# A decode kernel's first weight load in eight pieces of 16 partitions, and w3 in one load behind w2

## The chip, the cores and the metric

The kernel runs on one core of a Trainium2 chip (eight cores on two dies). The metric is the device time of the program in microseconds; the median of three runs before the change is 1324.46 us (1324.42 to 1324.49).

The core has five engines with a queue of instructions each: PE (TensorE, matrix products), DVE (VectorE), ACT (ScalarE), POOL (GpSimd) and SP (SyncE), which here only issues DMA transfers. The transfers run on 16 DMA engines of the core. SBUF is the working memory with 128 partitions; PSUM holds the results of PE.

## The reference

One decode step of two branches that are mixed by a gate. Branch A is attention of one query token against a long key and value cache, branch B a small gated mixer with two dense layers. The batch is 2, the model width 1024, there are 32 heads of 128 with 16384 cached positions each, and F is 3584. All inputs are bf16.

```
x = A_x                                            # [2, 1, 1024]
g = sigmoid((x * gate_w).sum(-1))

# A: q = x @ wq, attention over the caches, then @ wo
q = (x @ wq).reshape(B, 1, 32, 128)
scores = einsum(q, k_cache) * 128 ** -0.5
a = (softmax(scores) @ v_cache).reshape(B, 1, 4096) @ wo

# B: with one token, the shifted pieces of h are padding
h  = gelu(layernorm(x) @ w1)
x1 = x + shifted(h) @ w2
b  = x1 + gelu(layernorm(x1) @ w3) @ w4

out = g * a + (1 - g) * b
```

With one token per sequence every shift moves h out of the window, so shifted(h) is zero and w1 isn't read.

## The kernel before

All large operands go through one SBUF tensor, `ring`, of five slots with 128 partitions and 32 KB per partition each (`SLOT` is 16384 bf16 numbers). A block of the K or V cache is a pair of heads of one batch entry: 128 rows of 64 KB, which fills two slots. There are 32 such pairs, and so 32 K loads (L358) and 32 V loads (L362). V uses slots 0 and 1; K alternates between slots 2, 3 and 3, 4.

The weights use the same slots before the first pair: wq slots 0 and 1, w2 slot 2, w3 slots 3 and 4, and w4 slots 0 and 1 again once the q product has read wq. `runs` (L327 to L332) makes one such load: partition p gets rows r0 to r0 + rn of its own eight (or 28) rows of the weight, one contiguous run for each of the 128 partitions. wo comes behind the last V.

SP issues all ring loads, in the order of a list. `queue_load` appends to it and `pump` moves its head to SP's program as soon as the slots that it needs have a known release; the load then waits for the event that ends the last use of those slots. A load that is marked `more` takes slots that its predecessor already holds, and waits for nothing. The order before is: the first row of w3 for each partition (0.9 MB, key `("w3", "first")`), wq (8.4 MB), w2 (2.1 MB), rows 1 to 7 of w3 (6.4 MB, `more`), w4 (7.3 MB, waits for the q product), then K, V, K, V and so on. Each load adds to a semaphore of its first slot (`s_ring`) when it lands. Loads in several pieces, which only wo has, use one semaphore for each piece (`s_tail`).

On PE the prologue is fixed: the transposes of x (L587), the q product on wq (256 small matmuls, L602, which wait for all of wq), the permutation of q (L611), the gate, the product with w2 (L507), the layer norm, the product with w3 (L474, 224 matmuls), the gelu, and the product with w4 (L507, 112 matmuls). Each product waits for its whole weight. The K block of the first pair needs slots 2 and 3: w2's product and the first five of eight steps of w3's product release them. The loop then runs 16 times over two pairs each: DVE transposes K in place (L645), PE computes the scores (L651), DVE and ACT the softmax, PE the product with V (L687).

A few small loads of x and gate_w are issued by ACT at the start (L566 to L569).

## Time and profile before

| what | value |
|---|---|
| median of 3 runs | 1324.46 us |
| the profiled execution: span from the first to the last instruction | 1323.1 us |
| bytes read from HBM | 570.44 MB, 431 GB/s over the span |
| PE busy | 780.2 us (59%) |
| DVE busy | 659.8 us (50%) |
| ACT, POOL busy | 45.7 us (3%), 23.5 us (2%) |
| chain that ended last | DMA 71%, PE 23%, DVE 6% |
| mean granted clock of TensorE | 0.801 |

The profiled execution's own time is its span of 1323.1 us and what lies around it; the runs' median is 1.4 us above that span.

The page gives busy shares of 40 equal slices of the span (33.1 us each here), the chain that ended last, and groups of instructions. The timeline lists merged instructions: start, duration, engine, line, operands, and in brackets the idle time ahead of them and what ended it. The windows view gives busy times in chosen stretches. Where it books a DMA packet, it books it whole; a 64 KB packet lasts over 2 us, so short windows of the DMA column swing around the mean. In the trace "in_B_w_dram" stands for w2, w3 and w4 alike, since numbers in names are left out; the sizes tell them apart: 896 KB is the first row of w3, 2048 KB w2, 6272 KB the rest of w3, and 7168 KB w4. The wq load is one of 8192 KB.

### The profile page before, as it was taken

The page shows a single profiled execution, that of the slowest core. Times are in us where ns is not written, and L with a number is a line of the kernel's source. Part 1 is how long each engine was busy: PE and PEld are TensorE (multiplying, and loading weights), DVE is VectorE, ACT ScalarE, POOL GpSimd, SP SyncE. Part 2 cuts the span into 40 slices and gives each one's busy share as a digit, 9 for nine tenths or more (in the row PEclk, how much of TensorE's full clock was granted, in tenths as well). Part 3 has the DMA queues.
Part 4 walks back from the last instruction along what each step waited for, and adds up shares of the span by engine and source line. Part 5 has one row for each costly group of instructions (what it writes and reads, how often), then busy time and mean ns, then how long its engine had stood idle before and what let it go on. Part 6 is the DMA issues. An engine that isn't in the chain of part 4 may idle for free.

```text
span 1323.1 us, 12311 instructions
## 1 busy us (share of the span) xinstructions
PE 780.2 (59%) x5235; PEld 333.4 (25%) x5235; DVE 659.8 (50%) x527; ACT 45.7 (3%) x99; POOL 23.5 (2%) x110
## 2 busy tenths in 40 slices
PE   1745556656456665645666564567556557756556
PEld 1622222222222222222222222222222222222223
DVE  0254446655444665544466554446655445665444
ACT  0000000000000000000000000000000000000000
POOL 3000000000000000000000000000000000000000
PEclk9976788787788878678887867888786788778679
DMA  9999999999999999999999999999999999999998
GB/s 416 433 425 437 432 434 432 436 434 434 432 434 436 430 436 436 428 442 430 428 442 430 428 442 430 428 442 430 428 442 430 430 440 430 430 440 430 432 438 367
DMA packets 11122, 570.60 MB, mean 431 GB/s; under 512 B 1236, under 2 KB 1764, under 8 KB 2023
## 3 DMA queue, kind: packets, MB, share of 16 engines
q1 hardware_dynamic: 11080, 570.43, 99.7%
q8 instruction: 8, 0.13, 0.0%
q10 hardware_dynamic: 30, 0.01, 0.0%
q14 instruction: 4, 0.02, 0.0%
HBM read 570.44 MB, written 0.00 MB: 431 GB/s over the span
## 4 chain that ended last, share of the span: by engine, by line
DMA 71%; PE 23%; DVE 6%; issue 0%; SPq 0%
DMA ring<-in_A_k_cache_dram 65%; PE ps L651 22%; DVE ring L645 6%; DMA ring<-in_B_w_dram 3%; DMA ring<-in_A_wo_dram 2%; PE ps L474 1%; SPq L331 0%; PE ps L726 0%; DVE orow L755 0%
## 5 line engine op out<-in xcount | busy, mean ns | idle before, releaser
L651 PE MATMUL ps<-ring,Z 128*128 128x512 bf16 x2048 | 531.7, 417 | 390.5 <-DVE ring L645 389.8
L645 DVE STREAM_TRANSPOSE ring<-ring 128x2048 f32<-128x2048 f32 x256 | 565.2, 2276 | 276.6 <-DMA ring<-in_A_k_cache_dram 276.6
L651 PEld LDWEIGHTS ps<-ring,Z 128*128 128x128 bf16 x2048 | 202.0, 104 | 707.5 <-issue 465.2
L687 PE MATMUL ps<-ring,PT_sb 128*32 128x512 bf16 x2048 | 167.8, 501 | 4.6 <-DVE recip L678 4.6
L701 DVE SCALAR_TENSOR_TENSOR OT_sb<-ps,gT,recip 128x2 f32 x32 | 7.0, 220 | 203.4 <-PE ps L698 203.4
L687 PEld LDWEIGHTS ps<-ring,PT_sb 128*32 128x32 bf16 x2048 | 68.3, 122 | 90.2 <-issue 69.0
L672 ACT ACTIVATE P_sb<-ps,negm 128x512 bf16<-128x512 f32 x32 | 22.0, 687 | 1007.1 <-DVE negm L670 1007.1
L661 DVE TENSOR_REDUCE rA<-ps 128x1 f32<-128x512 f32 x32 | 22.1, 692 | 64.2 <-PE ps L651 64.2
L676 PE MATMUL ps<-rowsum,hsel 128*128 128x1 f32 x128 | 23.6, 288 | 38.0 <-ACT P_sb L672 38.0
L674 DVE STREAM_TRANSPOSE PT_sb<-P_sb 128x512 bf16<-128x512 bf16 x32 | 22.8, 712 | 27.0 <-ACT P_sb L672 27.0
L632 POOL TENSOR_TENSOR Z<-q_f,mask 128x8 bf16<-128x8 f32 x64 | 12.3, 227 | 1205.8 <-PE ps L651 1205.8
L676 PEld LDWEIGHTS ps<-rowsum,hsel 128*128 128x128 f32 x128 | 20.9, 233 | 40.7 <-ACT P_sb L672 40.7
L663 PE MATMUL ps<-ident,rmax_bf 128*1 128x128 bf16 x32 | 6.9, 217 | 33.1 <-DVE rmax_bf L662 33.1
L696 ACT ACTIVATE acc_sb<-ps 128x512 bf16<-128x512 f32 x32 | 19.1, 597 | 198.5 <-PE ps L687 198.5
L698 PE MATMUL ps<-dsel,acc_sb 128*128 128x2 bf16 x128 | 8.1, 167 | 22.5 <-ACT acc_sb L696 22.5
L602 PE MATMUL ps<-xT_bf,ring 128*128 128x2 bf16 x256 | 7.1, 165 | 21.6 <-DMA ring<-in_A_wq_dram 19.3
L474 PE MATMUL ps<-xn_bf,ring 128*128 128x2 bf16 x224 | 14.4, 202 | 1.6 <-DMA ring<-in_B_w_dram 1.6
L698 PEld LDWEIGHTS ps<-dsel,acc_sb 128*128 128x128 bf16 x128 | 5.3, 96 | 38.2 <-ACT acc_sb L696 38.2
L663 PEld LDWEIGHTS ps<-ident,rmax_bf 128*1 128x1 bf16 x32 | 2.5, 79 | 48.9 <-DVE rmax_bf L662 48.9
L474 PEld LDWEIGHTS ps<-xn_bf,ring 128*128 128x128 bf16 x224 | 14.3, 162 | 1.7 <-DMA ring<-in_B_w_dram 1.7
L664 DVE TENSOR_REDUCE m_sb<-ps 1x2 bf16<-1x128 bf16 x32 | 8.9, 279 | 9.9 <-PE ps L663 9.9
L670 DVE TENSOR_SCALAR negm<-ps,cAB 128x1 f32<-128x1 f32 x32 | 8.9, 277 | 9.2 <-PE ps L667 9.2
(98 smaller groups left out, 87.2 us busy)
## 6 DMA issues: line engine op xcount, KB each, us to landing
ring<-in_B_w_dram SPq DMA_DIRECT2D x1, 7168.0 KB, 28.0
ring<-in_B_w_dram SPq DMA_DIRECT2D x1, 6272.0 KB, 43.6
ring<-in_A_wo_dram SPq DMA_DIRECT2D x1, 4096.0 KB, 38.6
ring<-in_B_w_dram SPq DMA_DIRECT2D x1, 2048.0 KB, 28.4
ring<-in_A_wo_dram SPq DMA_DIRECT2D x1, 2048.0 KB, 22.4
ring<-in_A_wo_dram SPq DMA_DIRECT2D x1, 1024.0 KB, 24.5
ring<-in_B_w_dram SPq DMA_DIRECT2D x1, 896.0 KB, 4.6
ring<-in_A_k_cache_dram SPq DMA_DIRECT2D x32, 27.0
```

Of the source, the lines that this page charges most:

```text
L474: fn = lambda e, nb=nb, kl=kl: e.matmul(out_ps[:, nb, :], lhsT=cols(wv, kl, nb, nout), rhs=rhs_of(kl), start=False, stop=True, skip_group_ ...
L632: ev = pl.add("pool", lambda e, hp=hp: e.tensor_tensor(Z[:, :, ZO:ZO + P].rearrange("p t (i c) -> p t i c", c=32)[:, :, 2 * hp:2 * hp + 2, ...
L645: return pl.add("dve", lambda e: e.transpose(ap, ap), waits=(arrived(("k", n)),), sig=True)
L651: ev = pl.add("pe", lambda e, bp=bp: e.matmul(S_ps[:, 0:NCOL], lhsT=Z[:, bp, ZO - 2 * u:ZO - 2 * u + P], rhs=kv[:, :, bp // 2, :, bp % 2], ...
L661: e1 = pl.add("dve", lambda e: e.tensor_reduce(rA[:, :], S_ps[:, 0:NCOL], axis=AX.X, op=ALU.max), waits=(ev_S[n],), sig=True)
L663: e3 = pl.add("pe", lambda e: e.transpose(mt_ps, rmax_bf[:, :], ident[:, :]), waits=(e2,), sig=True)
L672: e7 = pl.add("act", lambda e: e.activation(P_sb[:, :], S_ps[:, 0:NCOL], ACT.Exp, bias=negm[:, 0:1], scale=scale, accum_out=rowsum[:, 0:1] ...
L674: e8 = pl.add("dve", lambda e: e.transpose(PT_sb[:, :], P_sb[:, :]), waits=(e7,), sig=True)
L676: e9 = pl.add("pe", lambda e, hp=hp: e.matmul(l_ps[:, hp:hp + 1], lhsT=hsel[:, hp, :], rhs=rowsum[:, 0:1], start=True, stop=True, skip_gro ...
L687: ev = pl.add("pe", lambda e, jj=jj, cg=cg: e.matmul(acc_ps[32 * cg:32 * cg + 32, 0:512], lhsT=PT_sb[:, 32 * jj:32 * jj + 32], rhs=vv[:, 4 ...
L696: e1 = pl.add("act", lambda e: e.activation(acc_sb[:, :], acc_ps[:, 0:512], ACT.Copy), waits=(ev_pv,), sig=True)
L698: e2 = pl.add("pe", lambda e, w=w: e.matmul(oT_ps, lhsT=acc_sb[:, w * P:(w + 1) * P], rhs=dsel[:, w, :], start=(w == 0), stop=(w == 3)), w ...
```

## The change

wq becomes the first load of the list and is issued as eight loads. Load j takes partitions j, j + 8, j + 16 up to j + 120, 16 rows of 64 KB, from the same rows of wq as before into the same places. All eight use the semaphore of slot 0, and the q product waits for the sum of all eight. w3's separate first row goes, and all eight rows of w3 come in one load, 57 KB per partition, behind w2. It now waits for its slots by the ordinary rule, and they are free at the start.

```
@@ pump @@
-                    dsem = s_ring[slots[0]] if len(fns) == 1 else s_tail[k]
+                    dsem = s_ring[slots[0]] if len(fns) == 1 or key[0] == "wq" else s_tail[k]
@@ wloads @@
-        wloads[("wq", 0)] = [runs(A_wq, HD, 0, NBD)]
-        wloads[("w3", 0)] = [runs(B_w3, F, 1, NBD - 1)]
+        wloads[("wq", 0)] = [lambda e, idx, j=j: e.dma_start(
+            ring[j:P:8, idx:, :].rearrange("p s m -> p (s m)")[:, 0:NBD * HD],
+            A_wq.rearrange("(p r) n -> p (r n)", p=P)[j:P:8, :]) for j in range(8)]
+        wloads[("w3", 0)] = [runs(B_w3, F, 0, NBD)]
@@ the list @@
-        queue_load(("w3", "first"), [runs(B_w3, F, 0, 1)], w_slots["w3"])
         for key in [("wq", 0)] + w_order:
-            queue_load(key, wloads[key], w_slots[key[0]], more=key[0] == "w3")
+            queue_load(key, wloads[key], w_slots[key[0]])
```

The order of SP's instructions from the start of the program, before the change (line, operation, target and source, partitions x elements, and the engine whose semaphore it waits for; e_pe is PE's):

```order
L331 DMA ring<-in_B_w3_dram 128x3584
L331 DMA ring<-in_A_wq_dram 128x32768
L331 DMA ring<-in_B_w2_dram 128x8192
L331 DMA ring<-in_B_w3_dram 128x25088
L331 DMA ring<-in_B_w4_dram 128x28672 [waits e_pe]
L358 DMA ring<-in_A_k_cache_dram 128x32768 [waits e_pe]
```

The same place of SP's program with the change:

```order
L341 DMA ring<-in_A_wq_dram 16x32768 x8
L331 DMA ring<-in_B_w2_dram 128x8192
L331 DMA ring<-in_B_w3_dram 128x28672
L331 DMA ring<-in_B_w4_dram 128x28672 [waits e_pe]
L360 DMA ring<-in_A_k_cache_dram 128x32768 [waits e_pe]
```

The small load of w3 at the head is gone, wq stands first as eight loads of 16 rows, and from w2 on the order is as it was. The first load that waits for anything is w4, before and after.

PE's instructions at the start of the program with the change (dr0 and dr2 are the semaphores of the loads into slots 0 and 2):

```order
L588 MATMUL ps0<-ident,xg_row 128x3 [waits e_pool,dgw,dmisc]
L588 MATMUL ps0<-ident,xg_row 128x3 x7
L603 MATMUL ps1<-xT_bf,ring 128x2 [waits e_dve,dr0]
L603 MATMUL ps1<-xT_bf,ring 128x2 x255
L612 MATMUL ps2<-q_sb,PermQ 128x64 [waits e_pool,e_dve]
L612 MATMUL ps2<-q_sb,PermQ 128x64 x3
L400 MATMUL ps5<-gin,ones_f 128x2 [waits e_dve]
L509 MATMUL ps2<-ring,shT_bf 2x256 [waits dr2]
```

Nothing moved on PE: these rows are those of before but for line numbers, and the q product still waits once, for all of wq.

## The prediction

> **What bounds the kernel now.** I read the page's slices first, then the windows of the loop, then the chain that ended last, and last the timeline of the first 85 us, since the change lies there.

> ```profile
> DMA  9999999999999999999999999999999999999998
> GB/s 416 433 425 437 432 434 432 436 434 434 432 434 436 430 436 436 428 442 430 428 442 430 428 442 430 428 442 430 428 442 430 430 440 430 430 440 430 432 438 367
> DMA packets 11122, 570.60 MB, mean 431 GB/s; under 512 B 1236, under 2 KB 1764, under 8 KB 2023
> ```

> The DMA row is 9 in all slices but the last. No slice is empty, and the rate leaves 425 to 442 GB/s only in the first slice (416) and the last (367). 570.60 MB at one rate is the whole kernel: the compute engines follow.

> ```profile
> 82.15:120.85 38.70, 24.67 (x139) 10.14 (x139) 20.24 (x15) 1.38 (x3) 0.38 (x2) 0.72 1.01 434
> 1243.19:1281.89 38.70, 23.49 (x139) 9.61 (x139) 20.18 (x15) 1.38 (x3) 0.38 (x2) 0.76 1.00 434
> ```

> These are the first and the last pass of the loop (the windows view: length, then busy time of PE, PE loads, DVE, ACT, POOL, then clock, DMA share and GB/s). Both take 38.70 us at 434 GB/s, with PE busy for 24 of the 38.7 us and DVE for 20. A pass loads one K and one V block, 2 x 128 rows of 64 KB. Over the 16 DMA engines that is 16 rows each, so **one row takes 38.70 / 16 = 2.42 us on its engine**, or 27.1 GB/s. The clock of TensorE was 0.72 and 0.76 in the two passes and changed nothing. What the kernel costs is therefore: when the first byte moves, how long each engine needs for its share, and what comes behind the last byte. Work on PE matters only where a load is issued so late that the queue runs dry.

> ```profile
> 0.74 0.40 SPq L331 DMA_DIRECT2D ring<-in_B_w_dram  x1
> 1.20 0.42 SPq L331 DMA_DIRECT2D ring<-in_A_wq_dram  x1
> 1.67 33.41 SPq L331 DMA_DIRECT2D ring<-in_B_w_dram  x3
> 25.25 5.87 PE L602 MATMUL ps<-xT_bf,ring 128*128 128x2 bf16 x214 [19.29 <-DMA ring<-in_A_wq_dram]
> 34.76 0.23 DVE L607 CAST q_sb<-ps 128x64 bf16<-128x64 f32 x1 [16.75 <-PE ps L602]
> 45.34 0.17 DVE L441 TENSOR_TENSOR xn_bf<-zc,mv 128x16 bf16<-128x16 f32 x1 [0.83 <-POOL mv L439]
> 45.91 14.36 PE L474 MATMUL ps<-xn_bf,ring 128*128 128x2 bf16 x224 [1.60 <-DMA ring<-in_B_w_dram]
> 54.97 0.33 SPq L358 DMA_DIRECT2D ring<-in_A_k_cache_dram  x1
> 62.84 4.91 PE L507 MATMUL ps<-ring,GT_bf 128*2 128x256 bf16 x112 [2.58 <-DMA ring<-in_B_w_dram]
> ...
> 82.17 17.67 DVE L645 STREAM_TRANSPOSE ring<-ring 128x2048 f32<-128x2048 f32 x8 [11.55 <-DMA ring<-in_A_k_cache_dram]
> ```

> This is the timeline of the prologue. The q product waits for wq until 25.25. Its end lets SP issue w4 (the last of the x3, which ends at 1.67 + 33.41 = 35.08), 10.8 us before the w3 load in front of it lands (45.91). K of the first pair is issued at 54.97, 7.9 us before w4 lands (62.84). So the queue has at least 7.9 us of work in it whenever PE is what releases the next load.

> **The change, part by part.** The bytes are the same: w3 loses its separate first row (0.9 MB) and has all eight in one load, and wq comes as 8 x 16 rows. A term is needed for each of four things.

> *Issues on SP.* Two issues (0.40 and 0.42 us, rows above) become eight ahead of w2. At 0.46 us from one start to the next (0.74 to 1.20), w2 is issued at about 0.74 + 8 x 0.46 = 4.4 us instead of 1.67. A load of 16 rows has one row per engine, at least 2.42 us of work, so each load is issued before its predecessor is through, and w2's turn comes behind 19 us of wq. Cost 0. It would show if an issue took over 2.42 us, six times what any takes here.

> *The start of the stream.*

> ```profile
> 1.00:1.50 0.50, 0.00 (x0) 0.00 (x0) 0.00 (x0) 0.00 (x0) 0.30 (x1) 1.00 0.00 0
> 1.50:2.00 0.50, 0.00 (x0) 0.00 (x0) 0.00 (x0) 0.00 (x0) 0.41 (x2) 1.00 0.91 133
> 2.00:2.50 0.50, 0.00 (x0) 0.00 (x0) 0.00 (x0) 0.00 (x0) 0.39 (x2) 1.00 0.68 133
> 2.50:3.00 0.50, 0.00 (x0) 0.00 (x0) 0.00 (x0) 0.00 (x0) 0.39 (x3) 1.00 1.02 287
> 3.00:3.50 0.50, 0.00 (x0) 0.00 (x0) 0.00 (x0) 0.00 (x0) 0.33 (x4) 1.00 0.82 330
> 3.50:4.00 0.50, 0.00 (x0) 0.00 (x0) 0.00 (x0) 0.00 (x0) 0.50 (x1) 1.00 0.95 401
> 4.00:4.50 0.50, 0.00 (x0) 0.00 (x0) 0.00 (x0) 0.00 (x0) 0.32 (x2) 1.00 1.05 444
> ```

> In half-microsecond windows the first load, with rows of 7 KB, comes up through 133, 133, 287, 330 and 401 GB/s. Against 434 it loses (5 x 434 - 1284) x 0.5 / 434 = 1.0 us. Wide rows and short issues can save nothing at all or this 1.0 us. I take 0.4 us, since the first access is as cold as before and only the spread of the sixteen starts should shrink.

> *w2 and w3 behind wq.* w2 moves ahead of all of w3, and w3's 50 KB and 7 KB pieces become one 57 KB row. The bytes on each engine are unchanged and the loads are queued back to back: 0. What waits for them moves with them. q now waits for 2.1 us less (0.9 MB at 434), and w3 lands where it did.

> *The eight loads of 16 rows.* This is the term that decides, and no row of the trace shows a large load of fewer than 128 partitions. From below: each row takes the 2.42 us that it took, 8 rows per engine are 19.4 us, and the term is 0. That this is what wq costs now is seen here:

> ```profile
> ring<-in_B_w_dram SPq DMA_DIRECT2D x1, 896.0 KB, 4.6
> ring<-in_B_w_dram SPq DMA_DIRECT2D x1, 2048.0 KB, 28.4
> ring<-in_A_wq_dram SPq DMA_DIRECT2D x1, 24.0
> ...
> 26.00:28.00 2.00, 2.00 (x81) 2.00 (x79) 0.00 (x0) 0.00 (x0) 0.00 (x0) 1.00 1.03 443
> ```

> The first load lands at 0.74 + 4.6 = 5.3, wq at 1.20 + 24.0 = 25.2, so wq takes 19.9 us, near the 19.4. From above: if a load's rows come in by half as many ways as there are engines, two rows share each way, a row takes 4.84 us, and wq costs 8 x 2.42 = 19.4 us more. Every pass stands at the same 16 x 27.1 GB/s whatever PE and DVE do beside it, and w2 with its rows of 16 KB, which lands at 1.67 + 28.4 = 30.1 and so fills the window from 26 to 28, runs at 443, about the same. That is the picture of sixteen fixed ways of 27.1 GB/s and not of one common limit that happens to be shared. If such a way ends at an engine, the new loads still use all sixteen. If it ends at a group of partitions, it depends on which partitions a load touches: 128 rows fill all ways evenly and hide the grouping, while partitions j, j + 8, j + 16 ... all agree in their low three bits, so a grouping that uses one of those bits leaves half of the ways idle, for four loads in a row. The nearest rows, those of wq in one load, stand at the lower end, but they are no evidence for it: 128 rows look alike in both cases. I take the upper end, +19.4 us, because the spacing of eight is even for one kind of way alone, blocks of eight partitions, and uneven for every kind that deals them out more finely. Both ends stay in the range.

> [...]

> *What hangs on it.* With +19.4, wq lands near 25.25 - 2.1 - 0.4 + 19.4 = 42.1. The q product to the end of the normalization then takes the 45.34 - 25.25 = 20.1 us that it takes now, so xn_bf is there at 62.2. w3 lands at 45.91 - 0.4 + 19.4 = 64.9, still later, so PE waits for w3 as it does now. w4's issue comes at 42.1 + (35.08 - 25.25) = 51.9, 13 us ahead of w3's landing; K's and w4's times move alike. The queue stays full, the delay is neither hidden nor made larger, and everything behind it moves by one amount.

> **The sum.** The profiled execution spans 1323.1 us; the median of 1324.46 lies 1.4 us above it, which I carry along. 1323.1 - 0.4 + 19.4 + 0 + 0 + 1.4 = 1343.5, that is 1.4% slower.

> **The rivals.**

> *The same pace with 16 rows.* The ways end at the engines, every row keeps 2.42 us, and only the start moves: 1324.46 - 0.4 = 1324.1, with bounds of 1323.4 (all of the 1.0 us is saved) and 1324.5. This also decides the other sign: nothing but the start can gain, and 1.0 us is under the 0.2% (2.6 us) that a measurement of this kernel can tell from no change. For it speaks that each load has one row for each of 16 engines, and that the queue is full. Against it speaks only the regular spacing.

> *Rows dealt by partition to engines.* If it is the engine that is fixed by the partition's low bits, loads 0 to 3 give two rows each to eight engines and loads 4 to 7 to the other eight. The second eight start when the fifth load is issued, 4 x 0.46 = 1.8 us later, but each still has eight rows. The stream ends up to 1.8 us later: 1324.46 + 1.8 - 0.4 = 1325.9, within 0.2%. [...]

> *Fewer ways still.* If eight partitions apart leaves a quarter of the ways, a row takes four times 2.42 us and wq costs 3 x 19.4 = 58 us more: 1382.

> *A real gain.* Above 2.6 us it would need something ahead of the loop that is idle now, and the first two slices have no room for it.

> **How the numbers follow.** Half the ways 0.63, the same pace 0.29, dealt by partition 0.04, a quarter 0.02, a gain 0.02. Slower by over 0.2% is 0.63 + 0.02 = 0.65, within 0.2% is 0.29 + 0.04 = 0.33, faster 0.02. The likeliest case has its own range of 1342 to 1346: the start between 0 and 1.0 us of gain, and up to 10% more than a doubling where two rows compete. Since the second case holds 0.29, the range must reach down to its lower bound: 1323.4 to 1346.

> **What would show it.** If the forecast is right, the q product starts near 42 us, the w3 product near 65 us, K of the first pair lands near 101, and the second slice of GB/s falls below 300, while every pass of the loop keeps 38.70 us at 434 GB/s. If the q product starts near 22.7 us and the first K lands near 82 as now, the term of the eight loads was nothing. If q starts at 42 but the end moves by less than 19 us, something behind it gave way that I take as rigid. If the passes themselves change length, my reading that they only follow the stream is wrong.

## The result, and the profile after

The kernel with the change takes 1345.83 us (median of 5 runs, 1345.75 to 1346.02) against 1324.42 us before (5 runs, 1324.26 to 1324.49): a ratio of 1.0162, 95% interval 1.015 to 1.0174, that is 21.4 us more. The profiled execution spans 1344.5 us, before 1323.1: the same 21.4.

The page of the changed kernel, its slices and its DMA totals (as quoted of before):

```profile
DMA  9999999999999999999999999999999999999998
GB/s 219 356 427 436 429 435 435 435 437 435 429 431 437 429 435 433 435 437 437 433 427 435 437 429 433 435 435 437 437 429 429 437 433 431 435 433 437 437 435 362
DMA packets 11089, 570.60 MB, mean 424 GB/s; under 512 B 1331, under 2 KB 1859, under 8 KB 1990
```

The bytes are the same 570.60 MB. The DMA engines are as busy as before, 9 in every slice, and yet the first slice has half the rate: 219 GB/s against 416. The busy share is made up of the packets' times, and a row of wq takes 5.1 us here instead of 2.42 (below): from 27 to 42 us the share is 0.99 at 202 GB/s. So the DMA row alone hides this loss; the GB/s row shows it. From the third slice on nothing differs.

The windows view of the changed kernel, three stretches of wq, then w2 and w3, then the first and the last pass of the loop (length, busy PE, PE loads, DVE, ACT, POOL, clock, DMA share, GB/s):

```profile
7.00:22.00 15.00, 0.61 (x8) 0.56 (x8) 2.64 (x11) 1.28 (x1) 5.59 (x25) 1.00 0.92 188
22.00:27.00 5.00, 0.00 (x0) 0.00 (x0) 0.00 (x0) 0.00 (x0) 0.00 (x0) 1.00 1.06 225
27.00:42.00 15.00, 0.00 (x0) 0.00 (x0) 0.00 (x0) 0.00 (x0) 0.00 (x0) 1.00 0.99 202
...
47.00:64.00 17.00, 8.60 (x205) 7.06 (x202) 5.24 (x18) 0.17 (x1) 0.13 (x1) 1.00 1.04 445
...
103.48:142.18 38.70, 23.49 (x139) 9.60 (x139) 20.18 (x15) 1.38 (x3) 0.38 (x2) 0.76 1.00 432
1264.52:1303.20 38.68, 23.35 (x139) 9.54 (x139) 20.18 (x15) 1.37 (x3) 0.38 (x2) 0.76 1.00 434
```

While wq comes in, the rate is 188 to 225 GB/s; with w2 and w3 it is 445, and a pass of the loop keeps its 38.7 us. The loss lies between 2 and 43 us, and all behind it is only later.

The timeline of the changed kernel at the places shown of before:

```profile
0.74 5.04 SPq L341 DMA_DIRECT2D ring<-in_A_wq_dram  x8
...
5.81 48.54 SPq L331 DMA_DIRECT2D ring<-in_B_w_dram  x3
...
44.14 5.87 PE L603 MATMUL ps<-xT_bf,ring 128*128 128x2 bf16 x214 [34.98 <-DMA ring<-in_A_wq_dram]
...
64.62 0.17 DVE L443 TENSOR_TENSOR xn_bf<-zc,mv 128x16 bf16<-128x16 f32 x1 [0.83 <-POOL mv L441]
67.25 14.35 PE L476 MATMUL ps<-xn_bf,ring 128*128 128x2 bf16 x224 [3.66 <-DMA ring<-in_B_w_dram]
76.31 0.33 SPq L360 DMA_DIRECT2D ring<-in_A_k_cache_dram  x1
...
84.19 4.74 PE L509 MATMUL ps<-ring,GT_bf 128*2 128x256 bf16 x112 [2.59 <-DMA ring<-in_B_w_dram]
...
103.51 17.67 DVE L646 STREAM_TRANSPOSE ring<-ring 128x2048 f32<-128x2048 f32 x8 [11.71 <-DMA ring<-in_A_k_cache_dram]
```

The q product starts 18.9 us later (25.25 to 44.14). Most of what is missing there to 21.3 is w3's first row, 2.1 us of work that came ahead of wq before. From the w3 product on everything is 21.3 us later: 45.91 to 67.25, 54.97 to 76.31, 62.84 to 84.19, 82.17 to 103.51.

The trace also holds each DMA packet with its start and duration; here a packet is one row of wq. Medians in us of the 1st to 16th row, the 17th to 32nd and so on, in order of their start:

```
change                              4.82 5.11 5.11 5.11 4.90 5.09 5.09 5.09
wq in one load of 128 partitions    3.06 2.42 2.42 2.42 2.42 2.42 2.42 2.42
```

(The second line is the first experiment.) In the change the first sixteen rows start between 2.14 and 2.83 us, so sixteen are under way at once, and from the second load on most take 5.1 us, 2.1 times the 2.42. The fifth load (j = 4) is a little faster, 4.90; this comes up again below.

### The profile page after: what moved, and what is told of

The parts are those of the page before. It is cut to its first block, busy times and chain, and to the rows that moved or that the text cites. A ratio compares the mean times of both kernels' runs of the same rounds, so it can differ in the third digit from the quotient of the medians.

```text
span 1344.5 us, 12301 instructions
## 1 busy us (share of the span) xinstructions
PE 792.1 (59%) x5235; PEld 336.1 (25%) x5235; DVE 659.7 (49%) x527; ACT 45.7 (3%) x99; POOL 23.5 (2%) x110
## 2 busy tenths in 40 slices
DMA  9999999999999999999999999999999999999998
DMA packets 11089, 570.60 MB, mean 424 GB/s; under 512 B 1331, under 2 KB 1859, under 8 KB 1990
## 4 chain that ended last, share of the span: by engine, by line
DMA 69%; PE 23%; DVE 6%; issue 1%; SPq 0%; another core or an unknown queue 0%
DMA ring<-in_A_k_cache_dram 64%; PE ps L652 22%; DVE ring L646 6%; DMA ring<-in_A_wq_dram 3%; DMA ring<-in_A_wo_dram 2%; PE ps L476 1%; PE ps L603 1%; SPq L341 0%; DVE hsd L543 0%; PE ps L509 0%; PE ps L400 0%; SPq L331 0%; DVE orow L756 0%; PE ps L727 0%
## 5 line engine op out<-in xcount | busy, mean ns | idle before, releaser
L688 PE MATMUL ps<-ring,PT_sb 128*32 128x512 bf16 x2048 | 179.6, 528 | 4.8 <-DVE recip L679 4.8
L677 PEld LDWEIGHTS ps<-rowsum,hsel 128*128 128x128 f32 x128 | 20.8, 231 | 40.7 <-ACT P_sb L673 40.7
L603 PEld LDWEIGHTS ps<-xT_bf,ring 128*128 128x128 bf16 x256 | 7.0, 104 | 37.9 <-DMA ring<-in_A_wq_dram 35.1
## 6 DMA issues: line engine op xcount, KB each, us to landing
ring<-in_B_w_dram SPq DMA_DIRECT2D x1, 2048.0 KB, 43.0
ring<-in_A_wo_dram SPq DMA_DIRECT2D x1, 2048.0 KB, 22.6
ring<-in_A_k_cache_dram SPq DMA_DIRECT2D x32, 27.1
ring<-in_A_wo_dram SPq DMA_DIRECT2D x1, 512.0 KB, 25.2
```

Of the source, the lines that this page charges most:

```text
L603: ev = pl.add("pe", lambda e, h=h, kc=kc: e.matmul(q_ps[:, h, :], lhsT=wv[:, kc, h * Dh:(h + 1) * Dh], rhs=xT_bf[:, kc, :], start=(kc == 0 ...
L677: e9 = pl.add("pe", lambda e, hp=hp: e.matmul(l_ps[:, hp:hp + 1], lhsT=hsel[:, hp, :], rhs=rowsum[:, 0:1], start=True, stop=True, skip_gro ...
L688: ev = pl.add("pe", lambda e, jj=jj, cg=cg: e.matmul(acc_ps[32 * cg:32 * cg + 32, 0:512], lhsT=PT_sb[:, 32 * jj:32 * jj + 32], rhs=vv[:, 4 ...
```

## The experiments

Three theories stood against each other. Landing: the engines' ways into SBUF end at groups of partitions, and rows that go to the same group share one. Spacing in HBM: rows read 512 KB apart collide at the source. Cost per load: a load of few rows has a cost of its own, 21.4 / 8 = 2.7 us. All kernels start from the changed one; only the list of wq loads differs, and `...` in an edit stands for parts left out. Where no count is given, the kernel ran once; the kernel before, run again beside each group of them, stayed between 1324.25 and 1324.66 us.

### wq in one load, the rest of the change kept

```
-        wloads[("wq", 0)] = [lambda e, idx, j=j: e.dma_start(ring[j:P:8, ...], ...[j:P:8, :]) for j in range(8)]
+        wloads[("wq", 0)] = [runs(A_wq, HD, 0, NBD)]
```

> wq stays first and w3 stays in one load, but wq comes in one load of 128 partitions. Landing theory (partition groups, half the ways): the 19 to 21 us are in the eight loads alone, so this is 1324.4 within 0.7 us; q product starts near 23. Spacing-in-HBM theory (rows 512 KB apart) and cost-per-load theory (2.7 us a load): the same, 1324. If the merging of w3 or the order has a share, it shows here as anything over 1325.5.

Measured 1324.52 us (10 runs) against 1324.42, ratio 1.0001, interval 0.9991 to 1.001. The order and the merging of w3 are worth nothing either way; the whole 21.4 us lie in the eight loads. It is what all three theories say, and it places the loss.

### Eight loads, each with all partitions

```
+        wloads[("wq", 0)] = [runs(A_wq, HD, k, 1) for k in range(NBD)]
```

> Eight loads of wq, each of all 128 partitions with an eighth of each row (8 KB). Landing theory: every load fills all ways evenly, 1324.4 within 1 us. Cost-per-load theory: 1346. Spacing-in-HBM theory: 64 KB between rows, 1324.

Measured 1324.93 us (10 runs), ratio 1.0004, interval 0.9994 to 1.0013. As many loads as the change, of the same 1 MB each, cost half a microsecond. A cost of a load as such falls. These loads have all 128 rows, so a cost of a load of few rows isn't tested here but in the next run.

### Half of each row in the eight loads

```
+        WH = NBD * HD // 2
+        wloads[("wq", 0)] = [runs(A_wq, HD, 0, NBD // 2)] + [lambda e, idx, j=j: e.dma_start(
+            ring[j:P:8, ...][:, WH:2 * WH], ...[j:P:8, WH:2 * WH]) for j in range(8)]
```

> Half of every wq row comes in one load of 128 partitions, the other half in eight loads of every eighth partition with rows of 32 KB. Landing theory: only the second half runs at half rate, 8 x (2.55 - 1.21) = 10.7 us more than in one load: about 1335. Spacing-in-HBM theory: also half the dose, 1335. Cost-per-load theory: eight loads as before, 1346.

Measured 1335.2 us, 10.8 more than before: half the bytes, half the loss, with all eight loads of 16 rows still there. A fixed cost of each such load would have given 1346, so that falls too.

### The same targets, contiguous sources

```
-            A_wq.rearrange("(p r) n -> p (r n)", p=P)[j:P:8, :]) for j in range(8)]
+            A_wq.rearrange("(p r) n -> p (r n)", p=P)[16 * j:16 * j + 16, :]) for j in range(8)]
```

> The change with its targets (every eighth partition) but source rows 16j to 16j+15, which are contiguous in HBM, so that the rows of wq land in a permuted order of partitions and q is that of a permuted wq. Landing theory: as the change, 1345.8. Spacing-in-HBM theory: no loss, 1324. Cost-per-load theory: 1346.

Measured 1345.86 us, the change's 1345.83. The spacing in HBM, 64 KB here and 512 KB there, plays no part in it.

### Contiguous blocks of 16 partitions

```
-            ring[j:P:8, idx:, :]...                ...[j:P:8, :]
+            ring[16 * j:16 * j + 16, idx:, :]...   ...[16 * j:16 * j + 16, :]
```

> Eight loads of 16 partitions as in the change, but load j takes the contiguous partitions 16j to 16j+15, from contiguous rows of wq. Landing theory: 16 contiguous partitions reach only 4 ways, four rows share one, a row takes about 4 x 2.55 = 10.2 us, wq 62 us more than in one load: about 1387. Spacing-in-HBM theory: the source rows are 64 KB apart, no loss, about 1324. Cost-per-load theory: as the change, 1346.

Measured 1379.55 us, 55.1 more than before. The windows of this kernel in the stretch of wq:

```profile
7.00:17.00 10.00, 0.62 (x8) 0.56 (x8) 1.67 (x9) 0.50 (x1) 5.65 (x25) 1.00 0.94 105
17.00:27.00 10.00, 0.00 (x0) 0.00 (x0) 0.97 (x2) 0.78 (x1) 0.00 (x0) 1.00 0.94 105
27.00:37.00 10.00, 0.00 (x0) 0.00 (x0) 0.00 (x0) 0.00 (x0) 0.00 (x0) 1.00 0.94 106
```

A quarter of 434 GB/s is 108. The sources are those of the kernel above, which took 1345.86; only the target partitions differ, and 34 us come of it. A row takes 9.32 us here, less than the 10.2 expected, and 8 x (9.32 - 2.42) = 55.2 gives the measured time. So the target partitions decide. Landing stands; the term for four rows on one way was too large by a tenth.

### Every seventh partition

```
+        wloads[("wq", 0)] = [... ring[p0:p0 + 15 * ps + 1:ps, ...], ...[p0:p0 + 15 * ps + 1:ps, :]
+            for p0, ps in [(j, 7) for j in range(7)] + [(112, 1)]]
```

> Seven loads of 16 rows with every seventh partition (j, j+7 ... j+105) and an eighth with the contiguous partitions 112 to 127. Landing theory with groups of four partitions and those 32 apart in one way: a stride of seven reaches 13 to 15 of the 16 ways, most rows of the first seven loads take 2.42 us and some 5.1, the last load reaches 4 ways; adding up rows by this map the slowest engine ends wq 10.6 us later than in one load, two engines hardly later: 1335 to 1337. Landing theory with blocks of another map: anything else. Cost-per-load theory: 1346. Spacing-in-HBM theory (448 KB here, and 64 KB): 1324 to 1345, no firm number.

Measured 1346.09 us, 10 us over what the landing theory gave by its map: a miss. The medians by sixteen rows, and all rows of the fourth load, in us:

```
medians        4.49 4.65 4.75 3.38 3.60 4.48 4.72 8.11
fourth load    3.73 3.73 3.56 3.63 3.44 4.77 3.41 3.35 3.27 3.25 3.21 3.14 4.75 2.98 2.96 2.88
```

The map (groups of four partitions, those 32 apart on one way) is an assumption here; no run up to this one shows it as a whole, and the last section has what the later runs add. By it the fourth load reaches 15 of 16 ways, so two of its rows share one and fourteen have their own. Two rows do stand out, 4.77 and 4.75, as the map has it. But the other fourteen take 2.9 to 3.7 us and not 2.42. The second and third load, rows 17 to 48, go further: by the map they reach 14 ways, so that twelve of their sixteen rows have a way of their own, and yet all sixteen take 4.6 to 4.8 us. Either rows that share nothing get slower beside rows that share, or the map is incomplete; this run doesn't decide between the two, and the cause stays open.

### Four loads of 32, every fourth partition

```
+        wloads[("wq", 0)] = [... ring[j:P:4, ...], ...[j:P:4, :] for j in range(4)]
```

> Four loads of 32 rows, every fourth partition. Landing theory: each engine takes two rows a load, and at any time its row shares a way with one other engine, so half rate as in the change: 1345.8 (if the two rows of an engine are neighbours in the load, or 16 apart, alike). Cost-per-load theory: half of the change's, 1335. Spacing-in-HBM theory: rows are 256 KB apart, no loss or less: 1324 to 1335.

Measured 1324.94 us: no loss at all, a second miss of the landing theory as I had put it. Rows take 2.42 us from the second on. I had assumed that an engine gets two neighbouring rows of the load (or rows 16 apart), with a collision in either case. At 2.42 us a row they can't collide, so they must be dealt out or staggered in some other way; the packets carry no engine, and no run here shows how. What is left of the theory is that a load runs at full rate if its partitions reach all ways. The next two runs test that with equal loads and rows.

### Two loads of 64, contiguous or spaced

```
+        wloads[("wq", 0)] = [... ring[64 * j:64 * j + 64, ...], ...[64 * j:64 * j + 64, :] for j in range(2)]
```

> wq in two loads of 64 contiguous partitions, 0 to 63 and 64 to 127. The four loads of 32 at every fourth partition cost nothing, against the forecast of the landing theory that took an engine's rows to be neighbours in the load. Landing theory as mended (what counts is how many of the 16 ways the partitions of one load reach, and the engines are dealt out so that they use all that are reached): 0 to 63 reach 8 of 16 ways, so half rate in both loads, 1345 to 1346. Rival, that only loads of as few as 16 rows are slow (one row per engine): 1324.5 to 1325.

```
+        wloads[("wq", 0)] = [... ring[j:P:2, ...], ...[j:P:2, :] for j in range(2)]
```

> wq in two loads of 64 rows, every second partition. Same number of loads, rows and bytes as in two contiguous halves, but all 16 ways are reached. Landing theory as mended: full rate, 1324.4 to 1325. If a load of fewer than 128 partitions is slow in itself unless it has 32 rows: over 1330.

Measured 1345.89 us with partitions 0 to 63 and then 64 to 127, and 1325.05 us with every second one. The windows of the first, then of the second:

```profile
7.00:17.00 10.00, 0.63 (x8) 0.58 (x8) 1.69 (x10) 0.59 (x1) 5.60 (x25) 1.00 0.93 190
17.00:27.00 10.00, 0.00 (x0) 0.00 (x0) 0.95 (x2) 0.69 (x1) 0.00 (x0) 1.00 1.01 211
```

```profile
7.00:17.00 10.00, 0.62 (x8) 0.57 (x8) 1.67 (x9) 0.54 (x1) 5.65 (x25) 1.00 0.97 419
17.00:27.00 10.00, 3.48 (x130) 3.49 (x131) 0.97 (x2) 0.74 (x1) 0.00 (x0) 1.00 1.03 442
```

Two loads of 64 rows each, and 20.8 us between them by which 64 it is. Neither the number of loads nor of rows in one decides, but which partitions a load touches. The windows have it as a rate: 190 to 211 GB/s for neighbouring partitions against 419 to 442 for every second one. Half the rate is what the expectation gives if either 64 neighbours reach half of the ways; the trace shows the rate and the time, not the ways.

### The eight loads in another order

```
-            ... for j in range(8)]
+            ... for j in (0, 4, 1, 5, 2, 6, 3, 7)]
```

> The eight loads of the change in the order j = 0, 4, 1, 5, 2, 6, 3, 7. Landing theory with bit 2 of the partition as one that chooses the way: at each of the seven borders between loads the engines that are ahead (by up to 1.2 us) use the other eight ways for that time; in the change only the border from load 3 to load 4 does, and its rows take 4.90 instead of 5.10 us. Seven such borders instead of one save 6 x 0.2 = 1.2 us: 1344.6, rows of 4.9 us in all loads but the first. Any theory in which bit 2 plays no part: 1345.8, rows of 5.1.

Measured 1344.74 us (4 runs), ratio 1.0153, interval 1.0136 to 1.017; the profiled spans are 1343.3 and, for the change, 1344.5. The 1.2 us were expected as 1.2. The medians by sixteen rows:

```
change          4.82 5.11 5.11 5.11 4.90 5.09 5.09 5.09
alternating     4.65 4.93 4.89 4.89 4.87 4.86 4.87 4.86
```

In the change one group of rows is near 4.90, at the border from j = 3 to j = 4; here all from the second on are. The reading put ahead of the run fits: loads 0 to 3 use one half of the ways and loads 4 to 7 the other, and an engine that is ahead across such a border has its new way with less company. A border from j to j + 4 changes bit 2 of the partition number; the forecast in which that bit plays no part was 1345.8, 1.1 us above what was measured. The ways themselves are not in the trace, so this stays a reading of the 4.90 and the 1.2 us.

### Sixteen loads of eight rows

```
+        wloads[("wq", 0)] = [... ring[p0:p0 + 29:4, ...], ...[p0:p0 + 29:4, :]
+            for p0 in [h + j for h in range(0, P, 32) for j in range(4)]]
```

> wq in 16 loads of 8 rows, every fourth partition of a block of 32: eight rows in eight different ways of one half, none shared. Landing theory: a row takes 2.42 us again, but only eight engines have one, so these carry 16 rows each, 38.7 us instead of 19.4: about 1344, as late as the change for another reason. If an engine is slow on any way other than the one that it has in a full load: rows above 2.42 us, above all for partitions 64 to 127, and over 1350. If small loads as such are slow: rows near 5.1 us and about 1387.

Measured 1360.12 us, above the 1344 of the landing theory and on the side of one of its rivals. The medians by eight rows, that is by about one load each:

```
3.08 2.42 2.42 2.44 2.43 3.03 2.42 2.42 4.57 5.11 5.10 5.06 5.04 4.24 2.42 2.42
```

The first eight loads go to partitions 0 to 63 and take 2.42 us a row (the 3.03 falls where the other engines begin w2). The next go to 64 to 127 and take 5.1, but the last two of those take 2.42 again. Two rows of its timeline and three of its windows view tell what differs:

```profile
11.61 54.03 SPq L331 DMA_DIRECT2D ring<-in_B_w_dram  x3
58.29 6.99 PE L604 MATMUL ps<-xT_bf,ring 128*128 128x2 bf16 x256 [51.27 <-DMA ring<-in_A_wq_dram]
13.00:20.00 7.00, 0.00 (x0) 0.00 (x0) 2.64 (x11) 1.28 (x1) 1.68 (x6) 1.00 0.95 376
...
24.00:30.00 6.00, 0.00 (x0) 0.00 (x0) 0.00 (x0) 0.00 (x0) 0.00 (x0) 1.00 0.95 194
...
48.00:54.00 6.00, 0.00 (x0) 0.00 (x0) 0.00 (x0) 0.00 (x0) 0.00 (x0) 1.00 0.36 131
```

w2 and w3 are issued from 11.61 on. Eight rows of wq are under way at a time, so eight engines have none (from 5 to 13 us the DMA share is 0.59, at 254 GB/s); these go on to their own rows of w2, from 14.0 us, and from 19.3 us to those of w3, packets of 57 KB. Beside the loads to partitions 0 to 63 this hardly slows anything but its beginning: from 13 to 20 the core moves 376 GB/s, wq's rows are back at 2.42, and w3's first eight packets take 2.12 us. Beside the loads to 64 to 127 both streams run at half rate: from 24 to 30 it is 194 GB/s, wq's rows take 5.1 and w3's packets 4.47. The last of these w3 packets ends at 51.0. Then the eight engines wait (the DMA share from 48 to 54 is 0.36), as w4 is not issued before the q product, and wq's rows, from 52.0 on, take 2.42 again. So neither these partitions nor the company of another load is slow in itself: the same two streams run at full rate or at half, depending on where wq's rows land. That the eight engines' own rows are those for partitions 64 to 127 is what the times fit, but the packets carry no address, so this part is an inference. The forecast had left out that the freed engines would go on to the next loads.

## Why the prediction was right

*What bounds the kernel.* Right: the loop keeps 38.7 us a pass, and the delay of the first 43 us passes to the end unchanged (21.3 at the first K, 21.4 at the end).

*Issues on SP.* Cost nothing, as said, though one comes every 5.04 / 8 = 0.63 us and not every 0.46, and w2 is issued at 5.81 and not 4.4. A row of 5.1 us leaves the queue full all the same.

*The start.* Wrong in sign. I had taken 0.4 us of gain. The windows of the changed kernel in the first microseconds, and the first issue as its chain of waits has it:

```profile
1.50:2.00 0.50, 0.00 (x0) 0.00 (x0) 0.00 (x0) 0.00 (x0) 0.41 (x2) 1.00 0.03 8
2.00:2.50 0.50, 0.00 (x0) 0.00 (x0) 0.00 (x0) 0.00 (x0) 0.39 (x2) 1.00 8.46 1835
...
0.74 0.62 SPq L341
```

Between 1.5 and 2.0, where 133 GB/s flowed before, there is almost nothing: the first packet starts at 2.14 us instead of 1.76. (A packet is booked whole where it starts, hence the 1835.) The first issue takes 0.62 us instead of 0.40, so this smaller load is not issued sooner. Its 16 rows alone are not the reason: the first load of 16 neighbouring partitions was issued in 0.39 us, with its first packet at 1.76. The sixteen first packets, whose spread was to shrink, start within 0.69 us of each other (2.14 to 2.83) against 0.50 before (1.76 to 2.26); that the first access is a cold one, no trace shows. Nor did the wide rows gain anything by themselves: the run with wq in one load is at 1324.52 against 1324.42. With 0.4 us of forecast gain and about 0.4 us lost, that term is 0.8 us off.

*w2 and w3 behind wq.* Right for the order and the merging, 0: the run with wq in one load is at 1324.52. Behind the eight loads, though, w2 takes 5.4 us instead of 4.9. Its first rows, up to 1.27 us long instead of 0.61, begin while wq's last rows are still under way. These 0.5 us were not in the sum.

*The eight loads.* Right in that their rows come in at half rate, mis-sized. Forecast were 19.4 us more for eight rows of 4.84 us. From the mean start of the first sixteen rows to the mean end of the last sixteen wq takes 40.4 us, against 20.0 in the run with wq in one load: 20.4 us more, since from the second load on a row takes about 5.10 us and not twice 2.42. The 1.0 us here, the 0.8 of the start and the 0.5 of w2 are the 2.3 us between 1343.5 and 1345.83. The time lies only 0.2 us inside the upper bound of 1346; the allowance of up to 10% over a doubling is what held the 5% that were measured. As far as the rows of before went, the choice of the upper end was a bet on the spacing, and no row bore it out. The two loads of 64 and the other order show it now, the first by 20.8 us between loads that differ only in their partitions. Of the low three bits that the prediction named, it is bit 2 that these runs point at: every eighth partition, with that bit the same in a whole load, takes 1345.83 us, and every fourth, with both values in each load, 1324.94.

*What hangs on it.* Right in order, each 2 us late like the term itself: q at 44.14 (42.1), the normalization at 64.62 (62.2), w3 still behind it at 67.25 (64.9). One sign was badly put: I wanted the second slice of GB/s below 300, and it is 356. wq ends near 43 us, 10 us into that slice of 33.6 us; the first slice with its 219 was the one to name.

*The rivals.* The same pace with 16 rows is refuted by the rows of 5.1 us. Rows dealt by partition to engines would have ended near 1325.9; it is refuted by that and by the first load, whose sixteen rows are all under way by 2.83 us. A quarter of the rate was measured, but for contiguous blocks (105 to 106 GB/s), not for every eighth partition.

No version here beats the kernel before: those that run wq at full rate are at 1324.5 to 1325.1.

## What to carry to other kernels

Of the loads of 16 rows and more, those of 128 partitions (1324.52 us) and of every fourth (1324.94) or every second one (1325.05) ran at full rate here; by the landing theory these reach all the ways into SBUF. Every eighth (1345.83) and either half of 64 (1345.89) got half, blocks of 16 (1379.55) a quarter, and every seventh (1346.09), which by the map misses only one or two of sixteen ways, was no faster than every eighth. Where a load like this one has to come in pieces, cut it by columns rather than by partitions (eight pieces by columns took 1324.93 us). And read the rate beside the busy share of the DMA engines, since the share stayed at 9 while the rate of the first slice went from 416 to 219 GB/s.

## What the runs showed of the hardware that was not expected

By this estimate a shared way does not move quite what an unshared one does. Taking the number of engines on a way from the map, two on one way take 5.10 us for a 64 KB row, which is 2 x 65.5 / 5.10 = 25.7 GB/s for the way; four take 9.32 us, 28.1 GB/s; one alone takes 2.42, 27.1 GB/s.

In a load in which only two rows share a way by the map, the other fourteen took 2.9 to 3.7 us instead of 2.42; in two loads with four such rows, all sixteen took 4.6 to 4.8. This made every seventh partition as slow as every eighth (1346.09 and 1345.83), although by the map nearly all ways are in use. The cause stays open.

Loads of 32 and 64 spaced rows ran at full rate, 2.42 us a row from the second on. By the landing theory their rows must reach the engines in an order that avoids sharing; which order that is, or whether there is one, no run here shows.
